# Key products of the first unit ahead of its gate: reordering the start of a local-attention and channel-mix kernel

## The chip, the cores and the metric

The kernel runs on one core of a Trainium2 chip. The metric is the time of one execution on the device in microseconds, given as the median of several runs. A profile is of one execution; its span runs from the first to the last instruction and is a little shorter than that execution's time.

The engines that matter here are TensorE (PE for matrix products, PEld for loading their stationary operand), VectorE (DVE), ScalarE (ACT), GpSimd (POOL) and SyncE (SP), which issues all transfers. Each works through its own queue in order; semaphores hold an instruction back until what it needs is there.

## The reference

Inputs are in 64-bit or 32-bit floats; the output is fp32 for 4 batches, 768 tokens, 512 features.

```python
# local attention: chunks of 32 queries, 16 keys to the left, 8 to the right, 8 memory keys
scores = scale * np.matmul(q_c, k_full.transpose(0, 1, 3, 2))
scores = scores - np.max(scores, axis=-1, keepdims=True)
a = np.exp(scores)
a = a / (np.sum(a, axis=-1, keepdims=True) + 1e-09)
out[:, :, c_start:c_end] = np.matmul(a, v_full)
...
# channel mix on x = attention output, x_prev = x shifted by one token
xk = mu_k * x + (1.0 - mu_k) * x_prev
xr = mu_r * x + (1.0 - mu_r) * x_prev
k = np.maximum(xk @ w_k, 0.0)
v = k * k @ w_v
r = 1.0 / (1.0 + np.exp(-(xr @ w_r)))
return (r * v).astype(np.float32)
```

w_k is 512 by 1024, w_v 1024 by 512, w_r 512 by 512.

## The kernel before, in words

The 3072 tokens are cut into 24 tiles of 128 (t) and 12 units of two tiles (u). For each unit the kernel runs these groups of TensorE work, named by letters in the code:

- s: scores of the unit's two tiles, 64 small products (L324). Then the softmax over 128 x 1024 numbers: maximum (L337), difference (L341) on VectorE, exponential (L349) on ScalarE, sum, a small addition and reciprocal (L353 to L355), normalisation (L359).
- t and a, one per tile: transposes of the weights (pt, L386), copied into a block layout (aTz), then the products with the values (px, L403), copied to xT.
- g, two per unit: the gate products with w_r (pr, L492), followed by a sigmoid on ScalarE (sg, L500), whose table has to be loaded, as has the exponential's after it.
- h, four per unit: the key products with w_k (ph, L531), each over all four row pieces of w_k and into one bank (tag "m", four of them). Then ReLU (L540), square (L547), high part (kh) and low part (kl, L557).
- v, four per unit: value products with w_v (pv, L588), two tiles by two halves of the contraction; the second half needs the second half of w_v. The result times the gate is o (L602), which is stored.

Between a and g or h stands the mix (prep): the difference to the shifted token (df, L451), two mixes on VectorE (L459; m = 1 for the receptance, then m = 0 for the key), and the split of each into a high and a low part (xh, xl, L475).

Products are made with pairs of rounded numbers: each operand is split into a high and a low part, and three products (high by high, high by low, low by high) are added up in one bank.

The weights arrive as 64-bit floats in ten pieces of 1 MB (two of w_r, four of w_k, four of w_v). Each takes five steps: ScalarE makes a scaled magnitude from the high words (mag, L270), VectorE shifts the low words (raw, L273) and joins both (L277), the high part is copied (by L228 on ScalarE or L230 on VectorE) and the low part is subtracted (L283). Loaded pieces and qk tiles share four buffers of the tag "big".

The order of work is not written out. A planner (class Plan) holds every step with a cost, the steps that it needs, its buffers and a due number. The due numbers of TensorE's groups come from te_order: a sequence that begins with LEAD and goes on unit by unit, each group later by the cost of the one ahead. The dues of other steps are worked back from those. The planner then takes, again and again, the step that can start earliest, the smaller due first on ties, and so writes the order of every engine's queue, the transfers on SP included. Where a step may run on several engines (either), it takes the one that ends first. In LEAD the first unit's scores, transposes, value products, the second scores and the first unit's gate (g0.0, g0.1) stand ahead of its first key product.

Until the first key product is issued, gaps of TensorE in the plan are filled with products into a bank called warm (L660, L663). Gaps worth over 25 products get, by their number, one of three lists of specially shaped ones (fill); smaller gaps get plain 128 x 128 products of zeros.

Of the kernel before, what the change touches and what calls it, by code (L numbers as in the profile page):

```python
# [31 lines left out]
LEAD = "s0 t0 t1 a0 a1 s1 g0.0 g0.1"  # L32
# [12 lines left out]
def woven(a):  # L45

    return a.rearrange("p (t n) -> p n t", t=2)
# [97 lines left out]
def te_order():  # L147

    nu = B * S // UTOK
    seq = LEAD.split()  # L150
    seq = [tuple([x[0]] + [int(n) for n in x[1:].split(".")]) for x in seq]
    for u in range(nu):
        a, b = 2 * u + 2, 2 * u + 3
        g = [("g", u + 1, c) for c in range(QPU)]
        h = [("h", u, f) for f in range(FT // 2)]
        v = [("v", u, c, n) for c in range(QPU) for n in range(2)]
        seq += h[:2] + [("t", a), ("t", b)] + h[2:3] + [("a", a), ("a", b)] + h[3:]
        seq += v[:1] + [("s", u + 2)] + g + v[1:]
    last = {"s": nu, "g": nu, "t": B * NQT, "a": B * NQT}
# [10 lines left out]
def local_attention__then__channel_mix(  # L170
# [44 lines left out]
    zero_r = const.tile([P, 2 * DM], F32R, tag="zeror", name="zero_r")  # L215
    nc.vector.memset(zero_sb, 0.0)
    nc.vector.memset(zero_r.bitcast(F32), 0.0)
# [21 lines left out]
    chunks = [(w_r, wr_hl, k) for k in range(KT // 2)]  # L239
    chunks += [(w_k, wk_hl, k) for k in range(KT)]  # L240
# [6 lines left out]
    def weight(i):  # L247
# [20 lines left out]
        def f_abs():  # L268
            m = T["mag", i] = sb("x4", [P, 2 * DM], f"mag{i}")
            nc.scalar.activation(m, word(1, F32), AF.Prelu, scale=TINY, alpha=-(2.0**32))  # L270
# [4 lines left out]
        def f_join():  # L275
            mi = T["mag", i].bitcast(U32)
            nc.vector.scalar_tensor_tensor(mi, mi, 3, word(0, U32), ALU.logical_shift_left, ALU.bitwise_or)  # L277

        def f_hi(e):
            copy(e, h, T["mag", i])  # L280

        def f_lo(e):
            e.tensor_sub(l, T["mag", i], h.bitcast(F32))  # L283

        raw, mag = Slot("big"), Slot("x4")
        a = op(("dma", 3.0), f_load, new=[raw])
        b = op(("act", 0.95), f_abs, [a], new=[mag], use=[raw])
        g = op(("dve", 0.62, True), f_low, [a], use=[raw])
        j = op(("dve", 1.15, True), f_join, [b, g], use=[raw, mag])
        hh = op(either(act=(0.95,), dve=(0.62, True)), f_hi, [j], use=[mag])  # L290
        ll = op(either(dve=(1.15, True), pool=(2.5, True)), f_lo, [hh], use=[mag])
# [10 lines left out]
    def scores(u):  # L302


        ts = range(u * QPU, (u + 1) * QPU)

# [5 lines left out]
        def f_s():  # L312
            s = T["s", u] = ps("s", f"s{u}", QPU)
            s5 = s.rearrange("p (h c r k) -> p h c r k", h=2, c=QPU, r=NPAIR)
            nq = NPAIR * NJ * CHUNK
            for c, t in enumerate(ts):
                a = T["qk", t]
                q4 = a[:, :nq].rearrange("p (r j q) -> p r j q", r=NPAIR, j=NJ)
                k4 = a[:, nq:].rearrange("p (r j k) -> p r j k", r=NPAIR, j=NJ)
                for r in range(NPAIR):  # L320
                    for j in range(NJ):
                        for h in range(2):
                            z = slice(64 * h, 64 * h + 64)
                            nc.tensor.matmul(  # L324
                                s5[CHUNK * j : CHUNK * (j + 1), h, c, r, :], q4[z, r, j, :], k4[z, r, j, :],
                                start=True, stop=True,
                            )

        def f_max():
            s5 = T["s", u].rearrange("p (h c r k) -> p h c r k", h=2, c=QPU, r=NPAIR)  # L330
            for c, t in enumerate(ts):
                if qts[t][1] == 0:
                    nc.vector.memset(s5[0:CHUNK, :, c, :, 0:LEFT], NEG)
                if qts[t][1] == NQT - 1:
                    nc.vector.memset(s5[P - CHUNK : P, :, c, :, LEFT + CHUNK : LEFT + CHUNK + RIGHT], NEG)
            mx = T["mx", u] = sb("sm", [P, NG], f"mx{u}")
            nc.vector.reduce_max(mx, T["s", u].rearrange("p (g k) -> p g k", k=NK), axis=AX.X)  # L337

        def f_sub():
            e = T["e", u] = sb("e", [P, NG, NK], f"e{u}")  # L340
            nc.vector.tensor_sub(  # L341
                e,
                T["s", u].rearrange("p (g k) -> p g k", k=NK),
                T["mx", u].unsqueeze(2).to_broadcast([P, NG, NK]),
            )

        def f_exp():
            e = T["e", u]
            nc.scalar.activation(e, e, AF.Exp, scale=SCALE)  # L349

        def f_sum():
            sm = T["sum", u] = sb("sm", [P, NG], f"sum{u}")
            nc.vector.reduce_sum(sm, T["e", u], axis=AX.X)  # L353
            nc.vector.tensor_scalar_add(sm, sm, 1e-9)
            nc.vector.reciprocal(sm, sm)  # L355

        def f_norm(g):
            e = T["e", u]
            g.tensor_mul(e, e, T["sum", u].unsqueeze(2).to_broadcast([P, NG, NK]))  # L359

        qs = [Slot("big") for _ in ts]
        s1, m1, m2, e = Slot("s"), Slot("sm"), Slot("sm"), Slot("e")
        ds = due["s", u]
        l = [op(("dma", 2.3), lambda t=t: f_load(t), new=[x]) for t, x in zip(ts, qs)]
        o_s = op(("pe", 1.6), f_s, l + [prior.get("s")], new=[s1], use=qs, due=ds)
        o_m = op(("dve", 1.15), f_max, [o_s], new=[m1], use=[s1], due=ds + 4)
        o_b = op(("dve", 1.15), f_sub, [o_m], new=[e], use=[s1, m1], due=ds + 5.5)
        o_e = op(("act", 1.0), f_exp, [o_b], use=[e])
        o_u = op(("dve", 1.55), f_sum, [o_e], new=[m2], use=[e])
        o_n = op(either(dve=(1.15, True), pool=(2.2, True)), f_norm, [o_u], use=[e, m2])  # L370
        prior.update(s=o_s)
        return o_n, e

    def attention(t, o_n, e):
# [54 lines left out]
        lv = op(("dma", 1.5), f_loadv, new=[vs])  # L429
# [14 lines left out]
    def prep(u):  # L444
# [9 lines left out]
        for m in (1, 0):  # L454
            def f_mix(m=m):
                d = T["df", u]
                f = T["xf", u, m] = sb("x4", [P, KT, UTOK], f"xf{u}") if m else d
# [19 lines left out]
            fs, hs, ls = Slot("x4") if m else ds, Slot(f"xh{m}"), Slot(f"xl{m}")  # L477
            o_d = op(("dve", 1.75, True), f_mix, [o_d, o_mu], new=[fs] if m else [], use=[ds, xslot[u]])
# [4 lines left out]
    def channel_mix(u):  # L483
# [38 lines left out]
        ks = []  # L522
        for f in range(FT // 2):
# [35 lines left out]
            s, kf, kh, kl = Slot("m"), Slot("kf"), Slot(f"kh{f}"), Slot(f"kl{f}")  # L559
# [4 lines left out]
            o1 = op(("pe", BLOCK), f_s1, deps, new=[s], use=list(mix[u, 0][2:]), due=dh)  # L564
# [48 lines left out]
    for u in range(NU):  # L613
        soft = scores(u)
        for t in range(u * QPU, (u + 1) * QPU):
            attention(t, *soft)
# [7 lines left out]

    def apart(t, d, cols=512):
        if cols == 2 * d:
            return t[:, :cols].rearrange("p (t n) -> p n t", t=2)
        return t[:, :cols].rearrange("p (o t n) -> p o n t", t=2, n=d)

    far = lambda t, cols: t.rearrange("p (t n) -> p n t", t=2)[:, : cols // 2]  # L630
    z, w = zero_r, wr_hl[0][0]
    zs, ws = z[:, :P], w[:, :P]
    four = z[:, :512].rearrange("p (t n) -> p n t", t=4)
    fill = {
        1: [(zs, far(z, 512), 5)] + [(zs, apart(z, d), 5) for d in (128, 64, 32, 16, 8)],
        2: [(ws, far(w, 256), 10)] + [(w.rearrange("p (n t) -> p n t", n=P)[:, :, 0], ws, 12)]
        + [(w[:, : t * P].rearrange("p (n t) -> p n t", t=t)[:, :, 0], ws, 12) for t in (2, 4)]
        + [(ws, far(w, P), 12)],
        3: [(zero_sb, woven(zero_sb), 8), (zs, four, 6), (zs, apart(z, 4), 5), (zs, apart(z, 2), 5)]
        + [(ws, apart(w, 128, 256), 10), (ws, apart(w, 256), 5)],  # L640
    }
    gap = 0
    with tc.manual_schedule():
        for o in plan.order():
            if o.eng == "pe":
                n = 0 if ("ph", 0, 0) in T else int((o.start - busy - 0.2) / (0.22 if busy else 0.43))
                if n > 0:
                    warm = warm or ps("m", "warm")
                if n > 25 and (gap := gap + 1) in fill:
                    for a, b, n in fill[gap]:  # L650
                        cols = 1
                        for x in b.shape[1:]:
                            cols *= x
                        d = warm[:, :cols]
                        if len(b.shape) == 3:
                            d = d.rearrange("p (n t) -> p n t", t=b.shape[2])
                        if len(b.shape) == 4:
# [59 lines left out]
```

## Time and profile before

| what | value |
| --- | --- |
| median of 3 runs | 421.47 us (420.61 to 421.57) |
| the profiled execution | 420.69 us |
| its span | 418.7 us |
| instructions | 10166 |
| TensorE products, busy | 409.4 us (98%) |
| VectorE busy | 261.7 us (63%) |
| ScalarE busy | 202.9 us (48%) |
| GpSimd busy | 15.8 us (4%) |
| HBM read, written | 42.01 MB, 6.29 MB |
| mean granted TensorE clock | 0.988 |

How to read the lines that follow: a row of a group gives the line of the kernel, the engine, the operation, output<-input by the program's names, shapes, a count, then busy time and mean duration of one in ns, then the idle time ahead of it and what ended it. In a timeline the first two numbers are start and length in us, and the bracket behind gives the idle time before and what ended it. In the chain of waits each row is start, length, and what the chain passes through. TensorE's busy share counts the warm products too, and the ends of products are modelled.

### The profile page before, as it was taken

What the parts mean: (1) busy time and instruction counts of PE and PEld (TensorE: products, weight loads), DVE (VectorE), ACT (ScalarE), POOL (GpSimd) and SP (SyncE); (2) the same over time, 40 slices, a digit from 0 to 9 for tenths busy, and PEclk for the clock granted to TensorE, in tenths of its full rate; (3) what the DMA queues carried; (4) which work ended last, traced back from release to release, by engine and by line L of the source; (5) the groups of instructions that cost most, each with busy time, mean ns of one, the idle gap of its engine ahead of it and who ended that gap; (6) DMA issues with size and microseconds to landing.
All of it is one profiled execution on the core that took longest, in us unless ns stands there. A gap on an engine that the chain in (4) does not pass through costs nothing.

```text
span 418.7 us, 10166 instructions
## 1 busy us (share of the span) xinstructions
PE 409.4 (98%) x4601; PEld 375.4 (90%) x4601; DVE 261.7 (63%) x351; ACT 202.9 (48%) x281; POOL 15.8 (4%) x22
## 2 busy tenths in 40 slices
PE   8979999999999999999999999999999999999996
PEld 8878898799899899899898898898898898998995
DVE  2888589948729639639639539539539449447121
ACT  1642878345545445455355355364364364363150
POOL 2000001001001001001001001001001001000000
PEclk9995999999999999999999999999999999999999
DMA  8996186413313314314205206205112012100101
GB/s 315 378 363 254 66 298 216 184 52 113 140 52 126 127 50 141 124 42 163 117 25 177 101 27 193 86 29 207 68 36 95 25 57 73 38 13 2 50 2 50
DMA packets 12906, 48.95 MB, mean 117 GB/s; under 512 B 1472, under 2 KB 1600, under 8 KB 12352
## 3 DMA queue, kind: packets, MB, share of 16 engines
q1 hardware_dynamic: 12864, 48.31, 31.6%
q8 instruction: 36, 0.59, 0.6%
q14 instruction: 6, 0.05, 0.0%
HBM read 42.01 MB, written 6.29 MB: 115 GB/s over the span
## 4 chain that ended last, share of the span: by engine, by line
PE 89%; DVE 5%; ACT 3%; DMA 1%; issue 1%; ACTq 0%; SPq 0%
PE pv L588 29%; PE ph L531 29%; PE pr L492 15%; PE px L403 5%; PE s L324 4%; PE warm L660 3%; PE pt L386 2%; PE warm L663 2%; DMA raw<-in_w_v_dram 1%; ACT mag L270 1%; DVE mag L277 1%; DVE raw L273 1%; DVE wvl L283 1%; ACT e L349 1%; ACT wkh L228 0%
## 5 line engine op out<-in xcount | busy, mean ns | idle before, releaser
L531 PE MATMUL ph<-xh,wkh 128*128 128x256 f32 x384 | 107.6, 280 | 0.0
L531 PE MATMUL ph<-xl,wkh 128*128 128x256 f32 x384 | 105.6, 275 | 0.0
L531 PE MATMUL ph<-xh,wkl 128*128 128x256 f32 x384 | 105.6, 275 | 0.0
L540 ACT ACTIVATE kf<-ph 128x512 f32<-128x512 f32 x48 | 28.7, 598 | 113.9 <-PE ph L531 110.2
L531 PEld LDWEIGHTS ph<-xh,wkh 128*128 128x128 f32 x384 | 73.6, 192 | 1.1
L531 PEld LDWEIGHTS ph<-xl,wkh 128*128 128x128 f32 x384 | 73.7, 192 | 0.3
L588 PE MATMUL pv<-wvh,kh 128*128 128x512 f32 x192 | 73.8, 385 | 0.0
L531 PEld LDWEIGHTS ph<-xh,wkl 128*128 128x128 f32 x384 | 73.7, 192 | 0.0
L588 PE MATMUL pv<-wvh,kl 128*128 128x512 f32 x192 | 72.8, 379 | 0.0
L588 PE MATMUL pv<-wvl,kh 128*128 128x512 f32 x192 | 72.8, 379 | 0.0
L557 DVE TENSOR_TENSOR kl<-kf,kh 128x512 fp32r<-128x512 f32 x38 | 26.3, 691 | 55.8 <-ACT kh L228 55.6
L602 DVE TENSOR_TENSOR o<-pv,sg 128x512 f32<-128x512 f32 x24 | 16.6, 690 | 45.1 <-PE pv L588 45.1
L588 PEld LDWEIGHTS pv<-wvh,kh 128*128 128x128 f32 x192 | 36.3, 189 | 5.5
L588 PEld LDWEIGHTS pv<-wvh,kl 128*128 128x128 f32 x192 | 36.3, 189 | 5.1
L588 PEld LDWEIGHTS pv<-wvl,kh 128*128 128x128 f32 x192 | 36.3, 189 | 4.6
L492 PE MATMUL pr<-wrh,xl 128*128 128x512 f32 x96 | 37.3, 388 | 1.0 <-DVE xl L475 1.0
L492 PE MATMUL pr<-wrh,xh 128*128 128x512 f32 x96 | 37.5, 391 | 0.0
L492 PE MATMUL pr<-wrl,xh 128*128 128x512 f32 x96 | 37.3, 388 | 0.0
L547 ACT ACTIVATE kf<-kf 128x512 f32<-128x512 f32 x48 | 30.3, 631 | 1.2
L228 ACT CAST kh<-kf 128x512 fp32r<-128x512 f32 x48 | 29.8, 622 | 1.5
L349 ACT ACTIVATE e<-e 128x1024 f32<-128x1024 f32 x12 | 12.7, 1057 | 34.7 <-DVE e L341 34.7
L459 DVE SCALAR_TENSOR_TENSOR df<-df,mu_sb,xT 128x256 f32<-128x256 f32 x48 | 29.2, 667 | 0.0
(63 smaller groups left out, 547.8 us busy)
## 6 DMA issues: line engine op xcount, KB each, us to landing
qk<-in_qk_dram SPq DMA_DIRECT2D x24, 768.0 KB, 5.8
vw<-in_vw_dram SPq DMA_DIRECT2D x24, 512.0 KB, 4.5
out_dram<-o SPq DMA_DIRECT2D x24, 256.0 KB, 2.0
raw<-in_w_k_dram SPq DMA_DIRECT2D x4, 1024.0 KB, 6.7
raw<-in_w_v_dram SPq DMA_DIRECT2D x4, 1024.0 KB, 6.8
raw<-in_w_r_dram SPq DMA_DIRECT2D x2, 1024.0 KB, 10.4
id_sb<-in_ident_dram SPq DMA_DIRECT2D x1, 64.0 KB, 6.4
mu_sb<-in_mu_dram SPq DMA_DIRECT2D x1, 4.0 KB, 11.6
```

The costliest lines, as they stand in the source:

```text
L228: e.copy(dst, src)
L324: nc.tensor.matmul(s5[CHUNK * j : CHUNK * (j + 1), h, c, r, :], q4[z, r, j, :], k4[z, r, j, :], start=True, stop=True,)
L349: nc.scalar.activation(e, e, AF.Exp, scale=SCALE)
L403: nc.tensor.matmul(p3[64 * h : 64 * h + 64, 2 * g : 2 * g + 2, CHUNK * j : CHUNK * j + CHUNK], v[:, g, h, j, :], a[:, h, g, j, :], start=True,
L459: nc.vector.scalar_tensor_tensor(f[:, k], d[:, k], mu_sb[:, m, k : k + 1], T["xT", u][:, k, :UTOK], ALU.mult, ALU.add)
L492: nc.tensor.matmul(pairs(p), x[:, k, c * P : (c + 1) * P], woven(w), start=(k + n == 0), stop=(k == KT - 1 and n == 2),)
L531: nc.tensor.matmul(pairs(p[:, i * UTOK : (i + 1) * UTOK]), w[:, fc], x[:, :, k].rearrange("p t n -> p n t"), start=(k + n == 0), stop=(k = ...
L540: e.activation(r, T["ph", u, f], AF.Relu)
L547: e.activation(q, q, AF.Square)
L557: e.tensor_sub(l, T["kf", u, f], T["kh", u, f].bitcast(F32))
L588: nc.tensor.matmul(pairs(p), x[:, tc_], woven(w), start=(f + n == 0), stop=(f == FT - 1 and n == 2))
L602: nc.vector.tensor_mul(o, T["pv", u, c], T["sg", u][:, c * DM : (c + 1) * DM])
```

## The change

- LEAD: the first scores are split into two groups by tile (s0.0, s0.1). The gate of the first unit moves behind its four key groups. The whole first unit is now written out in LEAD, and the loop starts at the second unit. The due numbers start at 6.0, not 8.0.
- The first unit's softmax runs by tiles: each step of it is done for one tile, then for the other. All other units keep whole steps; the code is the same function with n = 2.
- The weight pieces are planned with w_k first, then w_r, then w_v.
- The magnitude is written back over the high words of the loaded piece (no tile mag of its own). The tag "big" gets six buffers, "x4" three instead of four, "sm" four instead of two; the planned costs of transfers are set lower.
- The first unit's mix makes the key side (m = 0) first.
- The first unit's key products run by rows of w_k: one step per row piece k, into all four banks, 24 products each. The later units keep one step per bank.
- The filler is plain: every gap in the plan gets 128 x 128 products of zeros, and the tile zero_r with its clearing goes.

The core of the diff:

```diff
-LEAD = "s0 t0 t1 a0 a1 s1 g0.0 g0.1"
+LEAD = "s0.0 s0.1 t0 t1 a0 a1 s1.0 h0.0 h0.1 t2 t3 h0.2 a2 a3 h0.3 g0.0 g0.1 v0.0.0 s2.0 g1.0 g1.1 v0.0.1 v0.1.0 v0.1.1"
...
-    for u in range(nu):
+    for u in range(1, nu):
...
-    due, t = {}, 8.0
+    due, t = {}, 6.0
...
-        "big": 4, "vw": 2, "x4": 4,
-        "e": 1, "sm": 2, "xT": 2, "kf": 2, "sg": 2, "o": 3,
+        "big": 6, "vw": 2, "x4": 3,
+        "e": 1, "sm": 4, "xT": 2, "kf": 2, "sg": 2, "o": 3,
...
-    chunks = [(w_r, wr_hl, k) for k in range(KT // 2)]
-    chunks += [(w_k, wk_hl, k) for k in range(KT)]
+    chunks = [(w_k, wk_hl, k) for k in range(KT)]
+    chunks += [(w_r, wr_hl, k) for k in range(KT // 2)]
...
-            m = T["mag", i] = sb("x4", [P, 2 * DM], f"mag{i}")
-            nc.scalar.activation(m, word(1, F32), AF.Prelu, scale=TINY, alpha=-(2.0**32))
+            nc.scalar.activation(word(1, F32), word(1, F32), AF.Prelu, scale=TINY, alpha=-(2.0**32))
...
+        step = 1 if u == 0 else QPU
+        for c in range(0, QPU, step):
+            o_s, o_n = part(c, step, o_s, c == 0)
+            done += o_n
...
-        for m in (1, 0):
+        for m in (0, 1) if u == 0 else (1, 0):
...
+        def f_row(k):
+            xh, xl, (wh, wl) = T["xh", u, 0], T["xl", u, 0], wk_hl
+            for f in range(FT // 2):
+                if k == 0:
+                    T["ph", u, f] = ps("m", f"ph{u}_{f}")
+                p = T["ph", u, f]
+                for i in range(2):
+                    fc = slice((2 * f + i) * P, (2 * f + i + 1) * P)
+                    for n, (w, x) in enumerate(((wh[k], xh), (wh[k], xl), (wl[k], xh))):
+                        nc.tensor.matmul(
+                            pairs(p[:, i * UTOK : (i + 1) * UTOK]), w[:, fc], x[:, :, k].rearrange("p t n -> p n t"),
+                            start=(i + k + n == 0), stop=(k == KT - 1 and n == 2), skip_group_check=True,
+                        )
...
-                if n > 0:
+                for _ in range(n):
                     warm = warm or ps("m", "warm")
-                if n > 25 and (gap := gap + 1) in fill:
-                    for a, b, n in fill[gap]:
...
-                    n = 0
-                for _ in range(n):
                     nc.tensor.matmul(warm[:, :P], zero_sb, zero_sb, start=True, stop=True)
```

More of the change, by code (lines that the diff above doesn't have):

```diff
@@ L149, in te_order @@
     nu = B * S // UTOK
-    seq = LEAD.split()
-    seq = [tuple([x[0]] + [int(n) for n in x[1:].split(".")]) for x in seq]
-    for u in range(nu):
+    seq = [tuple([x[0]] + [int(n) for n in x[1:].split(".")]) for x in LEAD.split()]
+    for u in range(1, nu):
         a, b = 2 * u + 2, 2 * u + 3
@@ L275, in f_join @@
         def f_join():
-            mi = T["mag", i].bitcast(U32)
-            nc.vector.scalar_tensor_tensor(mi, mi, 3, word(0, U32), ALU.logical_shift_left, ALU.bitwise_or)
+            m = word(1, U32)
+            nc.vector.scalar_tensor_tensor(m, m, 3, word(0, U32), ALU.logical_shift_left, ALU.bitwise_or)
         def f_hi(e):
-            copy(e, h, T["mag", i])
+            copy(e, h, word(1, F32))
         def f_lo(e):
[L283 to L287, printed above, removed]
+            e.tensor_sub(l, word(1, F32), h.bitcast(F32))
+        raw = Slot("big")
+        a = op(("dma", 2.6), f_load, new=[raw])
+        b = op(("act", 0.95), f_abs, [a], use=[raw])
         g = op(("dve", 0.62, True), f_low, [a], use=[raw])
-        j = op(("dve", 1.15, True), f_join, [b, g], use=[raw, mag])
-        hh = op(either(act=(0.95,), dve=(0.62, True)), f_hi, [j], use=[mag])
-        ll = op(either(dve=(1.15, True), pool=(2.5, True)), f_lo, [hh], use=[mag])
+        j = op(("dve", 1.15, True), f_join, [b, g], use=[raw])
+        hh = op(either(act=(0.95,), dve=(0.62, True)), f_hi, [j], use=[raw])
+        ll = op(either(dve=(1.15, True), pool=(2.5, True)), f_lo, [hh], use=[raw])
         wdone[id(hi), k] = (hh, ll)
@@ L310, in f_load @@
             nc.sync.dma_start(a, qk[b, i])
[L312 to L355, printed above, removed]
@@ L371, in scores @@
+        qs = [Slot("big") for _ in ts]
+        l = [op(("dma", 2.1), lambda t=t: f_load(t), new=[x]) for t, x in zip(ts, qs)]
+        o_s, done = prior.get("s"), []
+        step = 1 if u == 0 else QPU
+        for c in range(0, QPU, step):
+            o_s, o_n = part(c, step, o_s, c == 0)
+            done += o_n
         prior.update(s=o_s)
-        return o_n, e
+        return done, es
     def attention(t, o_n, e):
@@ L453, in prep, with f_mix @@
         o_d = op(either(dve=(1.15, True), pool=(2.0, True)), f_df, deps, new=[ds], use=[xslot[u]])
-        for m in (1, 0):
-            def f_mix(m=m):
+        for m in (0, 1) if u == 0 else (1, 0):
+            last = m == (u == 0)
+            def f_mix(m=m, last=last):
                 d = T["df", u]
-                f = T["xf", u, m] = sb("x4", [P, KT, UTOK], f"xf{u}") if m else d
+                f = T["xf", u, m] = d if last else sb("x4", [P, KT, UTOK], f"xf{u}")
                 for k in range(KT):
@@ L475, in f_lo @@
                 e.tensor_sub(l, laid(), T["xh", u, m].bitcast(F32))
-            fs, hs, ls = Slot("x4") if m else ds, Slot(f"xh{m}"), Slot(f"xl{m}")
-            o_d = op(("dve", 1.75, True), f_mix, [o_d, o_mu], new=[fs] if m else [], use=[ds, xslot[u]])
+            fs, hs, ls = ds if last else Slot("x4"), Slot(f"xh{m}"), Slot(f"xl{m}")
+            o_d = op(("dve", 1.75, True), f_mix, [o_d, o_mu], new=[] if last else [fs], use=[ds, xslot[u]])
             o_h = op(either(act=(0.97,), dve=(0.61, True)), f_hi, [o_d], new=[hs], use=[fs])
@@ L522, in channel_mix @@
         ks = []
+        by_k = []
+        ms = [Slot("m") for _ in range(FT // 2)]
+        def f_row(k):
[7 more added lines that the diff above has]
+                    for n, (w, x) in enumerate(((wh[k], xh), (wh[k], xl), (wl[k], xh))):
+                        nc.tensor.matmul(
+                            pairs(p[:, i * UTOK : (i + 1) * UTOK]), w[:, fc], x[:, :, k].rearrange("p t n -> p n t"),
+                            start=(i + k + n == 0), stop=(k == KT - 1 and n == 2), skip_group_check=True,
+                        )
+        if u == 0:
+            for k in range(KT):
+                by_k.append(
+                    op(
+                        ("pe", BLOCK), lambda k=k: f_row(k), by_k[-1:] + list(mix[u, 0][:2]) + wdeps(wk_hl, [k]),
+                        new=ms if k == 0 else [], use=list(mix[u, 0][2:]) + ms * (k > 0), due=due["h", u, k],
+                    )
+                )
         for f in range(FT // 2):
@@ L563, in channel_mix @@
             dh = due["h", u, f]
-            o1 = op(("pe", BLOCK), f_s1, deps, new=[s], use=list(mix[u, 0][2:]), due=dh)
+            if u == 0:
+                o1 = by_k[-1]
+                dh = due["h", u, FT // 2 - 1] + 0.7 * f
+            else:
+                o1 = op(("pe", BLOCK), f_s1, deps, new=[s], use=list(mix[u, 0][2:]), due=dh)
             oa = op(either(act=(0.5,), dve=(0.61,)), f_relu, [o1], new=[kf], use=[s], due=dh + BLOCK + 1.5)
@@ L614, in local_attention__then__channel_mix @@
         soft = scores(u)
-        for t in range(u * QPU, (u + 1) * QPU):
-            attention(t, *soft)
+        for c in range(QPU):
+            attention(u * QPU + c, soft[0][c], soft[1])
     for u in range(NU):
```

110 lines of the change are left out of this document (65 added, 45 removed).

## The prediction

> **What bounds the kernel now.** I read the chain of waits first, in order of time, to see from where on TensorE is the only thing that counts.
>
> ```profile
> 25.02 11.08 PE warm L660 x58
> 36.10 7.47 PE pr L492 x24
> ...
> 45.49 1.06 ACT e L349
> 46.55 3.12 ACT mag L270 x3
> ...
> 75.63 5.02 PE pr L492 x22
> 80.65 5.18 PE pv L588 x24
> 85.83 5.36 PE ph L531 x48
> 91.19 0.87 PE pt L386 x8
> ...
> 94.74 2.02 PE px L403 x64
> ...
> 102.22 1.42 PE s L324 x89
> ...
> 414.86 0.02 issue
> ```
>
> Columns: start, length, engine, tile, line. From 75.63 to 414.86 the chain is TensorE without a hole. That is 339.2 us of products which this change neither removes nor shortens. All that can move lies ahead of 75.63. There the chain passes through 11.08 us of filler, gate products (pr) that take 7.47 us where 24 of the same kind of width (pv at 80.65) take 5.18, then the second exponential at 45.49. So I looked at ScalarE and VectorE in order of time in that stretch.
>
> ```profile
> 29.96 1.22 DVE L475 TENSOR_TENSOR xl<-xf,xh 128x1024 fp32r<-128x1024 f32 x1
> ```
> ```profile
> 34.62 1.28 ACT L500 ACT_TABLE_LOAD   x1
> 40.99 0.60 ACT L500 ACTIVATE sg<-pr 128x512 f32<-128x512 f32 x1 [5.09 <-PE pr L492]
> ```
> ```profile
> DVE sum L353 <- ACT e L349: 7.3, 2, 6.2
> DVE mx L337 <- PE s L324: 2.0, 1, 2.0
> ```
>
> The gate's last operand xl is ready at 31.2, but the filler holds TensorE until 36.1. ScalarE has by then taken the sigmoid (from 34.62) and waits in it, in order, 5.09 us. Behind it in ScalarE's queue stand the second softmax's exponential and the word work on the later w_k rows; VectorE, which needs both, stands 6.2 us. The next view gives busy time and clock by stretch (length; busy and count; clock; DMA).
>
> ```profile
> 8.90:75.63 66.73, 55.64 (x66) 0.92 0.73 271
> 75.63:85.83 10.20, 10.06 (x15) 1.00 0.23 93
> ```
> ```profile
> 24.25:30.22 5.97, 5.97 (x86) 1.00 0.98 377
> 30.22:40.46 10.24, 10.24 (x38) 0.50 0.61 230
> 40.46:75.63 35.17, 33.69 (x390) 1.00 0.60 215
> ```
>
> The first pair is VectorE: from its first softmax instruction to 75.63 it is busy 55.64 of 66.73 us and idle 11.1. The triple is TensorE: its clock is granted at half for 10.24 us, which stretches filler and gate. So the lead is a VectorE chain (ten weight pieces, two softmaxes, the mixes) with 11.1 us of holes, nearly all made by the filler, the gate and the in-order sigmoid.
>
> **The change, part by part.** I take the order from the due numbers in the code and the time from rows.
>
> *Gate behind the key products.* In the new LEAD h0.0 falls due at 13.7, g0.0 at 27.2 (before: g0.0 ahead of every h). w_k rows, the second softmax and the key mix therefore go ahead of w_r, the receptance mix and the sigmoid on SP, ScalarE and VectorE. The sigmoid no longer stands in front of the second exponential: the 6.2 us hole goes. What is late next is VectorE itself.
>
> *Softmax by tiles.* The first scores start when the first qk tile lands.
>
> ```profile
> 7.32 1.48 PE L324 MATMUL s<-qk 64*32 64x64 f32 x128
> ```
> ```profile
> DMA to landing us min/median/max: 4.2/7.8/10.9
> ```
> ```profile
> 0.74 0.86 SPq L310 DMA_DIRECT2D qk<-in_qk_dram  x2
> ...
> 8.21 0.95 SPq L310 DMA_DIRECT2D qk<-in_qk_dram  x2
> ```
>
> First issue 0.74 plus 4.2 is 4.95; half the scores take 0.74, so VectorE starts at about 5.9 instead of 8.9. The halves cost more than the whole:
>
> ```profile
> L337 DVE TENSOR_REDUCE mx<-s 128x16 f32<-128x1024 f32 x3 | 3.7, 1225 | 2.0 <-PE s L324 2.0
> L341 DVE TENSOR_TENSOR e<-s,mx 128x1024 f32<-128x1024 f32 x2 | 2.4, 1216 | 0.0
> L557 DVE TENSOR_TENSOR kl<-kf,kh 128x512 fp32r<-128x512 f32 x2 | 1.4, 696 | 0.0
> ```
>
> Two halves at 0.70 are 1.39 against 1.22, so 0.17 for each of four passes, and the two short instructions behind the sum come twice, which I put at 0.4 (estimate): 1.1 us in all.
>
> *Words in place, six load buffers.* The magnitude now stays in the raw tile. Same instructions, same sizes; the shift on the low word is strided the same way today. I cost it at nothing; six buffers cover the longer hold.
>
> *w_k first.* DMA order by due numbers: qk0, qk1, vw, w_k0, qk2, qk3, w_k1, mu, w_k2, w_k3, w_r. The bytes and the rate do not change.
>
> ```profile
> 12.58 1.14 ACT L270 ACTIVATE mag<-raw 128x1024 f32<-128x1024 f32 x1
> ```
>
> Today's first weight piece stands in the same place of the queue and is used at 12.58. Three transfers later w_k1 follows, about 2.62 MB at 400 GB/s (the 377 above is close), so near 19 us; VectorE, by the sum further down, reaches it at 22 or 23. Loads stay covered. Were that cover gone, each piece that is 1 us late would cost 1 us.
>
> *Rows of w_k into four banks.* The same 96 products (two times 5.36 us), in four groups of 24 that each wait for one row. Cycling banks every third product has no row here; its nearest is the scores, which go to another bank with each of 128 instructions and take 1.48 us, 12 ns each. I take no cost, at most 1 us.
>
> *Plain filler.* Fillers exist only ahead of the first key product. Between the second scores and row 0 the code's 0.22 us each makes some 28 zero products, about 6 us. VectorE needs until about 25 us to make row 0's operands. In passes of 1.22, a shift or a cast at half of that (estimates): first softmax 6.4, one weight piece 3.7, difference, mix and low part 4, the second softmax's first passes and a shift 3, holes 2; with the 5.9 that is 25.0. The filler lies beside that.
>
> *An instruction wait.*
>
> ```profile
> 24.25 0.76 PE L324 MATMUL s<-qk 64*32 64x64 f32 x53 [2.24 <-issue]
> ```
>
> TensorE stands 2.24 us in the middle of the second scores, though its tiles, issued from 8.21 to 9.16, had landed 10.9 us later at most, by 20.1. VectorE lost 2.0 to it. Whether it recurs is open: between 0 and 2.2, I take 1.
>
> **The sum.** Let T be the start of the product that stays last late, v0.0.1 (it needs the second half of w_v). In the due order VectorE has by then done all it does today before 75.63, plus these three, which it or GpSimd does about or after that:
>
> ```profile
> 75.81 1.22 DVE L337 TENSOR_REDUCE mx<-s 128x16 f32<-128x1024 f32 x1
> 76.95 0.68 DVE L557 TENSOR_TENSOR kl<-kf,kh 128x512 fp32r<-128x512 f32 x1
> 77.55 1.22 DVE L341 TENSOR_TENSOR e<-s,mx 128x1024 f32<-128x1024 f32 x1
> ```
> ```profile
> 66.04 1.33 POOL L557 TENSOR_TENSOR kl<-kf,kh 128x512 fp32r<-128x512 f32 x1 [62.94 <-ACT kh L228]
> ```
>
> T = 5.9 + 55.6 + 2.4 (third softmax's first passes) + 1.4 (two kl) + 1.1 (halves) + 2.0 holes (1 for the instruction wait, 1 early) = 68.4. From T on there remain v0.0.1 (half of 5.18, 2.6), v0.1.0 and v0.1.1 (80.65), and everything from 85.83: 414.86 - 80.65 + 2.6 = 336.8. The last product then ends at 405.2. The tail stays 3.84 (418.7 - 414.86), so the span is 409.0; the profiled execution's 420.69 stands 1.99 above its span, which makes 411.0. The profiled execution is 0.8 below the median of the three runs (421.47), within what runs differ by, so I leave 411.0. After T, h1.0 needs its mix within 3 times 2.6 = 7.8 us; the row 75.63:85.83 less the three above leaves 6.9 of VectorE work. It fits narrowly.
>
> Does TensorE itself fit before T? From row 0 it has 10.7 (h), 2.9 (pt, px), 10.4 (two gates), 1.4 (s) and 2.6 (v0.0.0): 28.0 us in the 43 from 25 to 68. It fits at full clock.
>
> [...] In the rows above the clock fell at 30.22, in a stretch where TensorE shows busy all 5.97 us, six microseconds after its longest hole of 2.24. [...]
>
> **The rivals.** *One clock drop.* The new lead has 15 us of holes in 43 and no filler after row 0; the gate has to wait some 3 us for w_r, v0.0.1 about as long. For it: today's drop came with busy filler, so weak activity is enough. Against: 33.69 busy of 35.17 ran at full clock. A drop of the length seen, 10.24 us at 0.50, loses 5.1: 416.1.
>
> *The sigmoid blocks again.* If the sigmoid stands on ScalarE ahead of casts that VectorE needs for w_v and the gate is late, the 5.09 us come back: 416.1 likewise. Against: the casts for w_v can also go to VectorE.
>
> *Better.* No instruction wait, 2 to 3 us of casts kept off VectorE, no early hole: T = 64, 406.6.
>
> *Slower.* The clock stays at half from row 0 to T. The 28.0 us then take 56: T = 25 + 56 = 81, 423.6. It becomes a loss from T = 78.1 on (420.69 - 1.99 - 3.84 - 336.8), which is when 25 of the 28 us run at half. For it: holes at every row, and a drop today without a hole at its place. [...] Against: no half-clock stretch here was longer than 10.24.
>
> *It does not do it.* The hole moves: w_k's rows wait for something else as long as the gate did, T near 78: 421.
>
> **How the numbers follow.** Forecast, T within 66 to 71, 0.58. Clock drop 0.17, sigmoid 0.08, better 0.08, slower 0.06, no effect 0.03. The range takes in the better case, the forecast and both single losses with 2 us for the bank cycling and the instruction wait: 405 to 418, about 0.85. A measurement of this kernel tells apart about 0.3%, 1.3 us. Faster by more than that: 0.91; within: 0.03; slower: 0.06.
>
> **What would show it.** First softmax instruction on VectorE near 6; no VectorE hole over 3 us between 10 and 65; sg after the last row of ph; first ph near 25 and the rows some 4 to 5 us apart; v0.0.1 near 68, and TensorE without holes from there. The forecast is wrong if the clock rows show 0.50 anywhere after 25, if ph starts after 30, or if VectorE shows over 5 us of holes.

## The result and the profile after

| what | before | after |
| --- | --- | --- |
| median, beside each other on one chip | 421.04 us (419.53 to 421.57, 4 runs) | 410.87 us (408.98 to 416.92, 4 runs) |
| ratio, 95% interval | | 0.9749 (0.9702 to 0.9796) |
| the profiled execution, its span | 420.69, 418.7 us | 411.12, 409.3 us |
| first key product of the second unit starts | 85.83 us | 78.10 us |

The change saves 2.5%, some 10 us; 411.0 had been forecast. Ratios, here and below, leave out disturbed runs (of the changed kernel the one of 416.92), while medians and ranges are of all runs.

The chain of waits of the changed kernel, in order of time (start, length, engine, tile, line):

```profile
14.79 2.88 PE warm L680 x24
...
18.10 1.16 PE s L336 x74
19.26 1.97 issue
...
44.07 2.57 DVE raw L273 x2
51.51 3.11 DVE raw L273 x2
...
72.72 5.38 PE pv L638 x24
78.10 5.36 PE ph L577 x48
...
395.13 10.38 PE pv L638 x48
```

Up to 21.75 the chain runs through TensorE: plain filler, the scores and a stop in the second scores ("issue"). From 21.77 to 71.20 it is VectorE, over half of it weight work, then the scores of the unit after next, and from 72.72 TensorE to the end. The last product ends at 405.51. From the second unit's first key product to the end of the span there are 418.7 - 85.83 = 332.9 us before and 409.3 - 78.10 = 331.2 after, so nearly all of the difference comes from ahead of it: 7.7 of 9.4 us. Of the other 1.7 us, 1.5 are the scores of the unit after next, which TensorE took behind that point before and takes at 71.24 now. All that the experiments compare is therefore the lead, the first 75 to 85 us, up to the second unit's first key product.

VectorE in the changed kernel by stretches (length; busy and count; clock; DMA share; GB/s):

```profile
6.89:72.72 65.83, 60.40 (x76) 0.97 0.80 309
```

It is busy 60.40 of 65.83 us. Before, it was 55.64 of 66.73. TensorE's clock, by the same view:

```profile
0.00:58.47 58.47, 49.61 (x810) 1.00 0.88 341
58.47:61.88 3.41, 3.41 (x10) 0.50 1.00 364
61.88:72.70 10.82, 10.01 (x169) 1.00 0.26 92
```

The half clock from 30.22 to 40.46 is gone; 3.41 us of it stand at 58.47, in the first value products. TensorE in order of time:

```profile
18.03 1.23 PE L336 MATMUL s<-qk 64*32 64x64 f32 x101
21.24 0.44 PE L336 MATMUL s<-qk 64*32 64x64 f32 x27 [1.97 <-issue]
21.61 1.15 PE L422 MATMUL px<-aTz,vw 128*64 128x64 f32 x32
22.69 9.20 PE L680 MATMUL warm<-zero_sb 128*128 128x128 f32 x80
31.64 0.36 PE L556 MATMUL ph<-xh,wkh 128*128 128x256 f32 x1
...
58.01 0.48 PE L638 MATMUL pv<-wvh,kh 128*128 128x512 f32 x1 [2.33 <-ACT sg L521]
```

The second scores (128 products for a unit's two tiles) stop in the middle again, for 1.97 us with no releaser that the profile shows. The first row of w_k starts at 31.64, after 9.20 us of plain filler. The first value product waits 2.33 us for the sigmoid, which holds the bank that it needs.

### The profile page after: what moved, and what is told of

The parts are those of the page before. It is cut to its first block, busy times and chain, and to the rows that moved or that the text cites. A ratio compares the mean times of both kernels' runs of the same rounds, so it can differ in the third digit from the quotient of the medians.

```text
span 409.3 us, 10120 instructions
## 1 busy us (share of the span) xinstructions
PE 395.8 (97%) x4576; PEld 363.8 (89%) x4576; DVE 260.2 (64%) x353; ACT 208.5 (51%) x285; POOL 17.9 (4%) x22
## 4 chain that ended last, share of the span: by engine, by line
PE 86%; DVE 11%; issue 2%; DVEq 0%
PE pv L638 30%; PE ph L577 29%; PE pr L513 13%; PE px L422 5%; PE s L336 4%; DVE raw L273 3%; PE warm L680 3%; PE pt L405 2%; DVE raw L269 1%; DVE wvl L279 1%; DVE wkl L279 1%; DVE xl L496 1%; DVE xf L480 1%; DVE mx L349 1%; DVE e L354 1%
## 5 line engine op out<-in xcount | busy, mean ns | idle before, releaser
L577 PE MATMUL ph<-xh,wkh 128*128 128x256 f32 x352 | 98.6, 280 | 0.0
L577 PE MATMUL ph<-xh,wkl 128*128 128x256 f32 x352 | 96.8, 275 | 0.0
L577 PE MATMUL ph<-xl,wkh 128*128 128x256 f32 x352 | 96.8, 275 | 0.0
L638 PE MATMUL pv<-wvh,kl 128*128 128x512 f32 x192 | 73.7, 384 | 0.0
L577 PEld LDWEIGHTS ph<-xh,wkh 128*128 128x128 f32 x352 | 67.5, 192 | 1.0
L577 PEld LDWEIGHTS ph<-xl,wkh 128*128 128x128 f32 x352 | 67.5, 192 | 0.3
L577 PEld LDWEIGHTS ph<-xh,wkl 128*128 128x128 f32 x352 | 67.6, 192 | 0.0
L513 PE MATMUL pr<-wrh,xh 128*128 128x512 f32 x96 | 36.5, 380 | 0.0
L603 POOL TENSOR_TENSOR kl<-kf,kh 128x512 fp32r<-128x512 f32 x10 | 15.3, 1533 | 301.5 <-ACT kh L225 301.5
L225 ACT CAST xh<-df 128x1024 fp32r<-128x1024 f32 x12 | 18.3, 1527 | 19.7 <-DVE df L480 19.7
## 6 DMA issues: line engine op xcount, KB each, us to landing
mu_sb<-in_mu_dram SPq DMA_DIRECT2D x1, 4.0 KB, 12.7
```

The costliest lines, as they stand in the source:

```text
L225: e.copy(dst, src)
L513: nc.tensor.matmul(pairs(p), x[:, k, c * P : (c + 1) * P], woven(w), start=(k + n == 0), stop=(k == KT - 1 and n == 2),)
L577: nc.tensor.matmul(pairs(p[:, i * UTOK : (i + 1) * UTOK]), w[:, fc], x[:, :, k].rearrange("p t n -> p n t"), start=(k + n == 0), stop=(k = ...
L603: e.tensor_sub(l, T["kf", u, f], T["kh", u, f].bitcast(F32))
L638: nc.tensor.matmul(pairs(p), x[:, tc_], woven(w), start=(f + n == 0), stop=(f == FT - 1 and n == 2))
```

## The experiments

The theory under test is the prediction's: the gain comes from the gate's place behind the key products, with the sigmoid out of the exponential's way, and from an earlier start of VectorE. Its rivals: the filler's new form alone does it, by itself or by the clock; or the rows of w_k, which start TensorE's real work sooner, do it.

The ladder first, worked out from the runs below: which parts carry the gain. Each ratio is to the kernel before on the same chip.

| kernel | median | ratio (95%) |
| --- | --- | --- |
| before, with plain filler | 413.09 | 0.9823 (0.9795 to 0.9851) |
| that, and gate behind, w_k first | 409.18 | 0.9729 (0.9694 to 0.9763) |
| that, and softmax by tiles | 409.22 | 0.9733 (0.9704 to 0.9762) |
| the whole change | 410.87 | 0.9749 (0.9702 to 0.9796) |

**Plain filler alone, in the kernel before.** In the filler's loop only this is left:

```diff
-                if n > 25 and (gap := gap + 1) in fill:
...
-                    n = 0
                 for _ in range(n):
                     nc.tensor.matmul(warm[:, :P], zero_sb, zero_sb, start=True, stop=True)
```

The tile zero_r and its clearing go too.

> The kernel before with plain filler alone, and without the tile of zeros that the shaped filler used. My theory: the shaped filler overran its gap and lowered the clock, so the gate began some 4.6 us late and took 2.3 us longer, and the in-order sigmoid passed this on. With some 31 plain products the gate should start near 31.5 and the sigmoid should release the second exponential near 39: about 415, 6 us of the 10. Rival (the gate's place is what counts, whatever the filler): 419 to 422, no change.

Measured: 413.09 us, 0.9823 (0.9795 to 0.9851). TensorE by stretches in this kernel:

```profile
24.00:30.00 6.00, 6.00 (x55) 1.00 0.99 403
30.00:48.00 18.00, 17.20 (x152) 1.00 0.69 246
```

No half clock at all. The gate starts at 29.72 (35.89 before) and takes 5.4 us, the first unit's second transposes start at 44.72 (51.85), the first key product at 47.69 (55.13). So 7 of the 10 us come from the filler, with the gate still in its old place. That the gain needs the gate's new place falls as a whole; it can be worth 3 or 4 us at most. VectorE's holes, too, shrink with the filler alone, here in 66 us from its first softmax on:

```profile
9.10:75.10 66.00, 63.37 (x79) 1.00 0.77 287
```
```profile
DVE sum L351 <- ACT e L347: 1.1, 1, 1.1
```

It stands 2.6 of 66 us (11.1 of 66.73 before), and its wait for the exponential, 6.2 us at its longest before, is 1.1, although the sigmoid still stands in front of the second exponential.

**Which part of the filler.** The kernel before, where only the list in front of the gate is changed, from 58 products, most with strided columns of w_r as stationary operand, to 32 wide ones with the same numbers, columns in order:

```diff
-        2: [(ws, far(w, 256), 10)] + [(w.rearrange("p (n t) -> p n t", n=P)[:, :, 0], ws, 12)]
-        + [(w[:, : t * P].rearrange("p (n t) -> p n t", t=t)[:, :, 0], ws, 12) for t in (2, 4)]
-        + [(ws, far(w, P), 12)],
+        2: [(ws, far(w, 512), 32)],
```

> The kernel before with one list of its filler changed: the second gap gets 32 products of 512 columns of the same w_r data (about 7 us at full clock), not 58 products of which 36 load strided columns. Theory now (that list is too long for its gap and too idle for the clock): no half clock in 25 to 41, the gate starts near 32 and the time comes to 413 to 415, as with plain filler. Rival one (real data in the filler draws the clock down): half clock remains, 419 to 421. Rival two (the other two lists matter too): 416 to 418.

Measured: 415.58 us, 0.9877 (0.9847 to 0.9906). TensorE in this kernel:

```profile
24.55:31.72 7.17, 7.17 (x39) 1.00 0.87 341
31.72:52.00 20.28, 18.34 (x136) 1.00 0.62 220
```

The clock stays full on the same real data, so neither the data nor a filler of real numbers as such lowers it, but the old list's form; its length doesn't either, since the dense one lasts 7.17 us and the clock fell 5.3 us after the old one's start (24.95 to 30.22). That gives 5 of the 7 us. The other two are not to be seen in the remaining lists: filler and gate take as long as with plain products (7.17 and 5.4 us), but start 1.8 us later (24.55 against 22.77), because the second scores stop in the middle here and did not there:

```profile
21.45 0.99 PE L324 MATMUL s<-qk 64*32 64x64 f32 x75
23.86 0.76 PE L324 MATMUL s<-qk 64*32 64x64 f32 x53 [1.43 <-issue]
```

**The shaped list in the changed kernel.** In the one gap of over 25 products stands the old second list, made from w_k (the operand that is there by then):

```diff
+    shaped = [(ws, far(w, 256), 10)] + [(w.rearrange("p (n t) -> p n t", n=P)[:, :, 0], ws, 12)]
...
+                if n > 25:
+                    for a, b, n in shaped:
...
```

> The changed kernel with the shaped list of the second gap put in place of the plain products in its one gap of over 25, made from the first row of w_k instead of w_r. Theory (the list lowers the clock, and in the new order VectorE does not wait for TensorE there): half clock for some 10 us from about 30, row 0 some 2 to 5 us later, 412 to 415. Rival (in the new order the filler is harmless): 410 to 411.

Measured: 416.62 us (413.22 to 420.27), 0.9874 (0.9812 to 0.9936).

```profile
26.34:36.58 10.24, 10.24 (x48) 0.50 0.94 372
36.58:53.65 17.07, 13.55 (x256) 1.00 0.55 183
53.65:57.06 3.41, 3.41 (x55) 0.50 1.00 354
```

The half clock comes back in the same length, 4.5 us after the list starts at 21.88, and with it about 5 us by the ratios, in runs that spread over 7. The list takes the clock down in both leads.

**No filler at all behind the first scores, in the changed kernel.**

```diff
-                n = 0 if ("ph", 0, 0) in T else int((o.start - busy - 0.2) / (0.22 if busy else 0.43))
+                n = 0 if ("ph", 0, 0) in T or busy else int((o.start - busy - 0.2) / (0.22 if busy else 0.43))
```

> The changed kernel without filler behind the first scores (the products ahead of them stay). Theory (filler matters through the clock alone): TensorE's clock is granted at half in several stretches before the rows have run for a while; scores, transposes and value products of the first unit take twice as long and pass that to VectorE: 413 to 417. Rival (in the new order VectorE covers it): 410 to 412.

Measured: 413.21 us, 0.982 (0.9776 to 0.9864).

```profile
10.51:20.75 10.24, 6.24 (x170) 0.50 1.02 415
24.16:34.40 10.24, 4.53 (x19) 0.50 1.03 409
51.47:54.88 3.41, 3.41 (x70) 0.50 1.02 411
```

Without filler the clock is at half three times, for 24 us together, and the kernel is 2 us slower by the medians, 3 by the ratios. So in this lead plain filler (0.9749) looks a little better than none, though the intervals touch, and the shaped list (0.9874) is worse: it holds TensorE until 33.7, at half clock, where plain filler lets the first row start at 31.64.

**Gate behind the key products, and nothing else but plain filler.** The kernel before with plain filler and with the order alone (the gate's place, w_k loaded first and the key mix first, which move together): softmax whole, key products by banks, four load buffers, the magnitude in its own tile.

```diff
-LEAD = "s0 t0 t1 a0 a1 s1 g0.0 g0.1"
+LEAD = "s0 t0 t1 a0 a1 s1 h0.0 h0.1 t2 t3 h0.2 a2 a3 h0.3 g0.0 g0.1 v0.0.0 s2 g1.0 g1.1 v0.0.1 v0.1.0 v0.1.1"
...
+    chunks = [(w_k, wk_hl, k) for k in range(KT)]
+    chunks += [(w_r, wr_hl, k) for k in range(KT // 2)]
...
+        for m in (0, 1) if u == 0 else (1, 0):
```

> The kernel before with plain filler and the gate behind the key products (sequence, w_k planned first, key mix first); whole softmax, bank by bank, four buffers, magnitude in its own tile. Theory of the prediction (the gate's place removes a VectorE hole): faster than plain filler alone by 2 to 4 us, 409 to 411 where that one stands at 413. Rival (after the filler is mended the place of the gate gives nothing): 413 plus or minus 1.

Measured: 409.18 us, 0.9729 (0.9694 to 0.9763), not to be told from the whole change. VectorE in its lead, and what it waited for up to its end (us, times, longest; the 7.1 lie ahead of the stretch):

```profile
8.11:74.11 66.00, 63.38 (x78) 1.00 0.84 314
```
```profile
DVE s L331 <- PE s L322: 7.1, 1, 7.1
DVE sum L351 <- ACT e L347: 1.1, 1, 1.1
```

The order is worth about 4 us beside plain filler (0.9823 to 0.9729). It isn't worth them by VectorE's holes, as the prediction had it: behind the first scores VectorE has 2.6 us of holes in 66 here, and as many with plain filler alone. What differs is what TensorE still has to do when VectorE's part of the chain ends. First with plain filler alone, then here:

```profile
66.81 1.15 DVE xl L473
...
68.00 5.02 PE pr L490 x22
73.01 5.18 PE pv L586 x24
```
```profile
69.14 1.15 DVE wvl L281
...
70.33 3.94 PE pv L588 x17
```

VectorE's part ends at 67.95 there and at 70.29 here, but then 10.2 us are left there before the second unit's first key product and 3.9 here. The second unit's gate (pr) stood behind VectorE's last instruction; here its low part xl is made at 59.74, not 66.69, and the gate runs at 61.81, ahead of the last of w_v. The first unit's key products start at 33.17 (47.69). The second scores come at 26.83 here and run through in 1.48 us.

**The gate in front again, in the changed kernel.** LEAD with g0.0 and g0.1 ahead of h0.0, w_r loaded first, receptance mix first.

```diff
-LEAD = "s0.0 s0.1 t0 t1 a0 a1 s1.0 h0.0 h0.1 t2 t3 h0.2 a2 a3 h0.3 g0.0 g0.1 v0.0.0 s2.0 g1.0 g1.1 v0.0.1 v0.1.0 v0.1.1"
+LEAD = "s0.0 s0.1 t0 t1 a0 a1 s1.0 g0.0 g0.1 h0.0 h0.1 t2 t3 h0.2 a2 a3 h0.3 v0.0.0 s2.0 g1.0 g1.1 v0.0.1 v0.1.0 v0.1.1"
...
-        for m in (0, 1) if u == 0 else (1, 0):
+        for m in (1, 0):
```

> The changed kernel with the first unit's gate put back ahead of its key products (sequence, receptance mix first, w_r planned first); rows into four banks, tiles, buffers and plain filler stay. My theory: the sigmoid stands again on ScalarE ahead of the second exponential, VectorE gets a hole of 3 to 5 us: 414 to 416. Rival (the filler was the whole loss, VectorE's total is the same in either order): 410 to 412.

Measured: 415.06 us, 0.9863 (0.9828 to 0.9898), 4.2 us behind the change. The size agrees with the run above, the mechanism isn't the one that I had in mind. What TensorE waited for:

```profile
PE ph L556 <- ACT sg L521: 5.4, 1, 5.4
```

The rows need all four banks "m" at once, and the gate holds its own until the sigmoid has read them; so here it is TensorE that stands behind the sigmoid. With the rows, the gate has to stand behind the key products.

**Key products by banks, in the changed kernel.** The switch for the first unit's rows is off.

```diff
-        if u == 0:
+        if False:
             for k in range(KT):
                 by_k.append(
...
-            if u == 0:
+            if False:
                 o1 = by_k[-1]
```

> The changed kernel with the first unit's key products bank by bank, each waiting for all four rows of w_k. They can then start only near 44 and end near 55 instead of 47. My theory (VectorE sets the lead, TensorE has room): 1 to 3 us slower, 412 to 414, since the gate and the value products follow later. Rival (the early rows are where the gain comes from): 8 us slower, 418 to 419.

Measured: 410.97 us, 0.978 (0.9743 to 0.9817), the same as the change. The rows start 5 us earlier than the banks do (31.64 to 36.91), and nothing comes of it; the first value product waits 2.4 us for the sigmoid in both kernels, and the second half of w_v is VectorE's. A large gain from the rows falls, so do the 1 to 3 us that I had expected to lose, and so does a cost of cycling the banks: a product of the rows takes 0.275 us, and one by banks 0.275.

**Softmax whole, in the changed kernel.**

```diff
-        step = 1 if u == 0 else QPU
+        step = QPU
```

The first scores are one group (s0.0) in LEAD, too.

> The changed kernel with the first softmax in whole steps over both tiles. My theory (VectorE's work sets the lead): VectorE starts 2 us later and saves 1.1 us of half steps, so 1 to 2 us slower: 412 to 413. Rival (the start is hidden behind the loads, since VectorE waits at 18 to 21 for the second scores anyway): 410 to 411, or below it by the 1.1 us saved.

Measured: 413.26 us (410.54 to 415.80), 0.9826 (0.9757 to 0.9896), inconclusive: two runs took 410.5 to 410.8 and two 415.7 to 415.8. In the profiled one (415.72) the second scores stop for 3.8 us ("issue") and the clock is at half twice:

```profile
20.28:27.11 6.83, 4.98 (x46) 0.50 1.00 405
61.24:68.06 6.82, 5.84 (x13) 0.50 0.89 358
```

**Softmax by tiles, asked again in a lead where the second scores don't stop.** The changed kernel without rows, magnitude in its own tile, four load buffers: the run with the gate behind, plus the tiles.

```diff
-        "big": 6, "vw": 2, "x4": 3,
+        "big": 4, "vw": 2, "x4": 4,
...
+            m = T["mag", i] = sb("x4", [P, 2 * DM], f"mag{i}")
...
```

> The changed kernel with key products bank by bank, the magnitude in its own tile, and the buffers of before (four and four): so plain filler, the gate behind and the softmax by tiles. Against plain filler and gate behind alone (409.2) it has the softmax by tiles. The prediction's term (start 3.0 earlier, 1.1 of half steps): 407 to 408. Rival one (the start is lost again in the wait for the second scores): 409 to 410. Rival two (the halves are what makes the changed kernel slower than those two parts alone): 411 or more.

Measured: 409.22 us, 0.9733 (0.9704 to 0.9762), the same as without tiles. VectorE's lead in it, from its first softmax instruction to the second unit's first key product:

```profile
6.90:74.59 67.69, 65.56 (x83) 1.00 0.79 294
```

It starts 1.2 us earlier than without tiles (8.11), but does 65.56 us of work where the other does 63.38. The halves explain at most 1 of these 2.2 us (four passes, each 1.3 to 1.4 for two halves against 1.22, and the short instructions twice); the rest is other work, among it one low part xl of 1.2 us that GpSimd takes in the other kernel. The early start is used up on the way.

**The low parts kl of the first unit on VectorE alone.** In the changed kernel GpSimd takes two of them:

```profile
64.12 4.60 POOL L603 TENSOR_TENSOR kl<-kf,kh 128x512 fp32r<-128x512 f32 x2 [61.02 <-ACT kh L225]
```
```profile
64.44 1.89 DVE L273 SCALAR_TENSOR_TENSOR raw<-raw 128x1024 uint32<-128x1024 uint32 x1
...
67.70 2.35 DVE L279 TENSOR_TENSOR wvl<-raw,wvh 128x1024 fp32r<-128x1024 f32 x1
```

In the kernel before one kl took GpSimd 1.33 us; here they take 2.3 each, and VectorE's own instructions take 1.89 and 2.35 beside them. The low part takes 1.2 elsewhere; the join takes 1.2 in the first pieces, but 1.76 at 61.78 too, with GpSimd idle. The edit:

```diff
+            if u == 0:
+                o3 = op(("dve", 0.62, True), lambda f_lo=f_lo: f_lo(nc.vector), [o2], new=[kl], use=[kf, kh])
...
```

> The changed kernel with the first unit's four low parts of k on VectorE only. Two of them ran on GpSimd from 64.1 to 68.7, while VectorE's join took 1.89 and its low part 2.35 instead of 1.22. Theory (GpSimd and VectorE hold each other up): VectorE pays 1.4 for the two and gets 1.8 back: 0 to 1 us faster, 410 to 411. Rival (GpSimd's help is free): 1.4 us slower, 412 to 413.

Measured: 414.50 us (410.28 to 416.82), 0.9825 (0.9776 to 0.9874). In the profiled run TensorE loses more than in the changed kernel at the second scores (3.9 us, 1.97 there) and at the third, which wait for their transfer (3.2 us, 1.8 there):

```profile
PE s L336 <- issue: 3.9, 1, 3.9
PE s L336 <- DMA qk<-in_qk_dram: 3.2, 1, 3.2
```

So this run can't say what the collision costs. The same edit on the kernel with plain filler and the gate behind:

> The kernel before with plain filler and the gate behind the key products (the fastest so far, 409.2, ratio 0.973) and with the first unit's low parts of k on VectorE only. Theory: 0 to 1 us below that, 408 to 409. Rival (GpSimd's help is free): 410 to 411.

Measured: 408.72 us, 0.9737 (0.9699 to 0.9775), no difference from that kernel (0.9729). But there the two kl took GpSimd 2.52 us together, 1.26 each, so little of a collision was there to be taken away: the join beside them took 1.93, and 1.52 without them. By an estimate from these rows the collision lengthens VectorE's work in the changed kernel by 2.35 - 1.2 for the low part and between 1.89 - 1.76 and 1.89 - 1.2 for the join, 1.3 to 1.8 us; by how much the time, stays open.

**Filler in the late holes of the changed kernel**, to take away the half clock at 58.47: plain products in TensorE's gaps between the last px and the second unit's gate, into a bank of their own tag.

```diff
...
+                if ("px", 3) in T and ("pr", 1, 0) not in T:
+                    n = int((o.start - busy - 0.2) / 0.22)
+                    if not late:
+                        warm, late = ps("tp", "late"), True
```

> The changed kernel with plain products also in the planned gaps between the second unit's value products and its gate, into a bank that rests there (4, 9 and 9 products). Theory (the one half-clock stretch at 58.5 comes from the sparse window before it; VectorE's last w_v piece at 72.3 sets the end of the lead): clock stays full, time falls by 0 to 1 us, 410 to 411. Rival (the half clock costs its full 1.7 us): 409. If the half clock stays although the gaps are filled, the sparse window is not its cause.

Measured: 414.67 us, 0.9836 (0.9786 to 0.9885). The profiled execution took 411.08, the others 414.5 to 415.1. In the profiled one the half clock is gone:

```profile
38.00:58.00 20.00, 19.16 (x304) 1.00 0.83 304
58.00:71.00 13.00, 10.38 (x50) 1.00 0.37 145
```

And yet the second unit's first key product starts at 77.67, and at 77.94 by the same view in the changed kernel: the time is VectorE's. So in the one execution that was profiled, the half clock in that place is worth 0.3 us at most. The other executions are 3 to 4 us slower and have a lower granted clock, 0.989 to 0.992 against 0.998; where in them it fell, and why, is open, as no trace of them exists.

## Why the prediction was right, and where it was not

**The number and the direction** were right: 411.0 forecast, 410.87 measured. That they agree so closely is luck, as the two errors below show. The view that the lead is a chain of VectorE work was right from 21.77 us on.

**VectorE's work** up to the last late value product: 60.5 forecast, 60.40 measured. The total agrees better than its parts: the ten joins take 14.8 us (12.5 before) and w_v's low parts 6.1 (4.7), while two of the four kl, 1.4 us in the sum, went to GpSimd.

**Its start and its holes** were mis-sized. It starts at 6.89, not 5.9, and has 5.4 us of holes, not 2.0. The largest is here, in VectorE's order of time:

```profile
21.77 1.23 DVE L349 TENSOR_REDUCE mx<-s 128x16 f32<-128x1024 f32 x1 [2.95 <-PE s L336]
```

It waits for the second scores, which stand 1.97 us in the stop that I had called an instruction wait and put at 1 out of 0 to 2.2; the profile shows no releaser for it. So T is 72.7, not 68.4: 4.3 us late, of which 1.0 is the start, 3.4 the holes, and -0.1 the work.

**What remains from T** was mis-sized the other way. I let v0.1.0 (2.59 us) and the scores of the unit after next (1.48) follow T; TensorE does both ahead of it, in holes that it has anyway. 332.8 us remain instead of 336.8. The two errors cancel to 0.3 us, so the forecast was closer than its steps.

**The filler** is the step that was mis-told. I priced it at nothing ("the filler lies beside that") and gave the gain to the gate's and the sigmoid's order. The run with plain filler alone has 7 of the 10 us, some 2 of them with the stop in the second scores, which is absent in it. "The sigmoid no longer stands in front of the second exponential: the 6.2 us hole goes" names a true hole and the wrong cure: with plain filler alone it is 1.1 us, the sigmoid still in front. The order brings 4 us more, and not by that hole: TensorE has 3.9 us left when VectorE's chain ends, not 10.2. The filler's size was off as well: not 28 products in about 6 us, but 80 in 9.20, 0.115 us each where the plan counts 0.22. The prediction had the rows in hand. It named filler and half clock as what stretched filler and gate, and by its own price for 10.24 us at half clock (5.1) it could have had most of those 7 as a term of their own.

**Softmax by tiles** brings nothing. The forecast had 3.0 us of an earlier start less 1.1 for the halves; in the lead without the stop the two versions are 0.9729 and 0.9733.

**Rows into four banks, at no cost**: right (0.275 us a product either way); and no gain either (410.87 and 410.97).

**In place and six buffers, at nothing**: not isolated. The ten joins take 14.8 us in the changed kernel and 13.5 and 12.7 in the two kernels with a magnitude tile of its own; GpSimd's collision explains up to 0.7 of that (1.89 - 1.2, an estimate). The whole change is not faster than the two kernels without them.

**First row near 25**: wrong, 31.64. The low part of the key mix was ready at 31.45, 6.4 us late: 1.0 by VectorE's start, 3.2 by its holes (5.2 up to there, not 2.0), and 2.2 by its work, since the order of the due numbers put work on the next w_k pieces ahead. The prediction had set "ph after 30", "0.50 after 25" and "over 5 us of holes" as signs against itself. All three came, and the time came out as forecast: the first two lie off the path (by-bank products 5 us later cost nothing; in the one execution profiled without the late half clock 0.3 us at most were gained), the third was paid for by the products done early.

**The clock.** In the changed kernel it fell at 58.47, behind a hole of 2.33 us; in the kernel before at 30.22, six us behind its longest one of 2.24; without filler at 24.16, in the middle of a hole of 6.8 us (21.80 to 28.63), 2.4 us into it. All the profiles of this case together have 13 falls up to TensorE's last product. Eleven come in a hole of TensorE of 2.08 to 6.83 us or at most 2 us behind one; the other two are those on the shaped list. Two holes of over 2 us, of 2.24 and 3.21, and all of 1.97 or less brought none. So the length of a hole alone doesn't tell whether the clock falls: one of 2.08 (without filler) has a fall in it, and one of 3.21 (low parts on VectorE) brought none. The rival of one clock drop did appear, but with a third of the length that I had given it and in a place where VectorE is the limit, so its 5.1 us did not.

## What to carry to other kernels

A filler is work on the path whenever the next real product could start: price its length and its clock by themselves before a gain is given to the order of the work, and try the plainest filler first. Where one engine's chain sets the end of a stage, the stage ends with that chain plus what another engine still has to do behind it. Work or holes taken off the chain shorten it, and so does work that the other engine can do before the chain ends; moving work that was never left over brings nothing, as the rows of w_k show. A forecast that comes out right should still be checked term by term, since here an error of 4.3 us and one of 4.0 cancelled.

## What the hardware showed

- Half clock came in lengths of 3.41 us (the changed kernel), 6.83 (softmax whole) and 10.24 (the kernel before), one, two and three times 3.41.
- The clock fell while TensorE showed as busy, at 30.22 in the kernel before and at 26.34 with the shaped list in the changed one. In the kernel before its last 3.02 us at full clock held 20 strided products of 128 columns:

```profile
27.20:30.22 3.02, 3.02 (x20) 1.00 1.00 381
```

  That is 0.15 us each, where the plain products of the changed kernel take 0.115 (80 in 9.20 us) and the dense list moves 512 columns in 0.22 (32 in 7.17). Whether the fewer columns per us took the clock down is not shown.
- TensorE stood 1.0 to 3.95 us without a releaser in the middle of the second scores in eight of the profiles, while the transfers ran at some 390 to 430 GB/s. Counted from the start of the program, the stop comes behind 348 to 351 products in all eight, though the products ahead of it differ: behind 349 in the kernel before, with 53 of the 128 scores left, and behind 349 in the changed one, with 27 left. Two other kernels, whose second scores come at 26 and 27 us, behind filler, pass that place and stop behind 476 and 477 products (2.17 us in the filler, 0.75 in the scores), some 128 further on. So, where it came, the stop goes with the place in TensorE's stream of instructions and not with the scores or their data. What TensorE waits for there is not shown: the cause wasn't tried by itself, and four kernels show no such stop at either place.
- GpSimd and VectorE took longer over some work that they did beside each other: a low part took GpSimd 1.33 us in the kernel before and 2.3 in the changed one, and one of VectorE's beside it 2.35 instead of 1.2. In the kernel with the gate behind, a VectorE instruction of 0.17 us took 1.82 beside a GpSimd subtraction of 2.42:

```profile
70.81 2.42 POOL L475 TENSOR_TENSOR xl<-df,xh 128x1024 fp32r<-128x1024 f32 x1 [5.80 <-ACT xh L226]
```
```profile
71.44 1.82 DVE L352 TENSOR_SCALAR sum<-sum 128x16 f32<-128x16 f32 x1
```

  What holds them up is not shown.
